# Early gate weight transposes, bias rows, and long rows for four divided zero fills, in a decode backward kernel

## The chip, the cores and the metric

The kernel runs on one core of one Trainium2 chip. The metric is device time in microseconds (us); lower is better. There is a profile of one execution of each kernel.

A run is labelled "slow" where it takes over 1.5% longer than the fastest run of the same kernel.

## The reference

The reference is one decode step of attention and a gate, with all gradients. Cut to what matters:

```
xn = layernorm(x)                               # x: 2 x 1 x 512
s  = attention(xn @ wq, last 4096 keys) @ wo    # 32 query heads, 8 KV heads, cache of 32768 keys
g  = silu(relu(xn @ w1 + b1)**2 @ w2 + b2)      # gate: 512 -> 1792 -> 512
out = x + s * g
# returned: out and the gradients of x, k_cache, v_cache, wq, wo, w1, b1, w2, b2
```

The gradients of the two caches have the cache's full shape (2 x 8 x 32768 x 128 bf16, 134 MB each), but only the last 4096 of 32768 keys are used. The other seven eighths, 235 MB, are zeros that must be written. That is most of what the kernel does.

## The kernel before

Zeros are written by 31 "fills" of 7.34 MB issued from GpSimd and one last fill from SyncE. The source is a tile of `uint8` zeros, cast during the transfer. A row longer than 28,672 bytes is written as fp32, so that a row of 57,344 bytes still fits the source:

```
def zf(o, q, r0, nent, rows, rep=1):       # nent x rep rows of rows*256 bytes each
    ...
    w = rows * DH
    if w > ZG * DH:                        # ZG = 112, DH = 128
        v = v.bitcast(F32); w //= 2
    ...
    sw_fill.append(nc.gpsimd.dma_start(out=v, in_=zs))

zlong = (0, 1, 3, 5, 7, 9, 11, 12, 14, 16, ...)     # whole fills: 128 entries of 224 rows (57,344 B), 1 packet each
zshort = {                                          # divided fills: (entries, rows of 256 B, repeats); last piece: what remains, one row each
    2: ((5, 8, 2), (120, 68, 3), (128, 32, 1), (16, 1, 1)),
    4: ((3, 1, 2), (2, 99, 6), (128, 112, 1), (128, 102, 1), (86, 1, 1)),
    ...
    13: ((2, 20, 2), (3, 30, 2), (128, 112, 1), (128, 109, 1), (124, 1, 1)),
    ...
}
```

Loads go out from SyncE: w1, w2, wo, wq, then the first V. The first K load shares its buffer with w1 and w2, so it waits until the gate weights have been transposed, which the old kernel does last in its prologue:

```
b1_bf = pw.tile([P, FK], BF16); dma_store.dma_start(out=b1_bf[:], in_=B_b1.rearrange("(p j) -> p j", j=FK))
b2_bf = pw.tile([P, DK], BF16); dma_store.dma_start(out=b2_bf[:], in_=B_b2.rearrange("(p k) -> p k", k=DK))
...   # layer norm, gate, dS;  do = dS @ wo.T;  q = xn @ wq
jobs = [...]                              # 112 transposes of w1 and w2 into w1T, w2T
...
knat = load(A_k_cache, 0, "k")            # the buffer of w1 and w2
for r in range(NR):                       # 4 rounds
    scores(dp_ps, vnat, zdo); scores(s_ps, knat, zq)
    ...                                   # softmax, its gradient
    outer_store(p_bf, bddo, vnat, out_3, r);  vnat = load(A_v_cache, r + 1, "v")   # dV written over V, stored
    outer_store(ds_bf, bdq, knat, out_2, r);  knat = load(A_k_cache, r + 1, "k")   # dK likewise
```

So in each round the next V (or K) can be loaded only when the gradient in the same buffer has been stored. At the end come the weight gradients; SyncE stores `out_8`, then `out_6`, and only then issues the last fill:

```
last = nc.sync.dma_start(out=out_6..., in_=dw1_st)
with tc.issue_after(last.ins):
    fin = nc.sync.dma_start(out=v, in_=zs)     # also waits for the last but one software fill
```

## Time and profile before

| | before |
|---|---|
| time, median | 765.2 us |
| span of the profiled run | 763.3 us |
| bytes moved, mean rate | 326.73 MB, 428 GB/s |
| PE, DVE, ACT busy | 51%, 36%, 28% |

The page of the kernel before: its span, the busy time and share of each engine, then two rows of 40 equal time slices (DMA in tenths busy, and GB/s), and the DMA packets.

```profile
span 763.3 us, 9400 instructions
PE 387.6 (51%) x4118; PEld 233.5 (31%) x4118; DVE 275.8 (36%) x483; ACT 214.6 (28%) x313; POOL 34.0 (4%) x67
DMA  9999999999999999999999999999999999999998
GB/s 382 443 416 422 451 412 425 444 435 416 430 432 450 416 439 429 426 427 446 414 431 435 437 428 427 429 433 440 425 436 437 432 434 422 428 441 425 422 428 379
DMA packets 11833, 326.73 MB, mean 428 GB/s; under 512 B 2898, under 2 KB 2906, under 8 KB 2934
```

No compute engine is near full; the DMA engines are, in every slice but the last. The GB/s jump from slice to slice; spread over their own durations, the packet records give 423 to 435 GB/s in every 10 us from 10 to 760 us.

What SyncE waited for before its first K load, in the view of waits (us in total, times, longest):

```profile
SPq L210 <- PE tp L345: 82.9, 1, 82.9
```

And why the layer norm starts so late, in the timeline (the bracket has the idle time before, and what ended it):

```profile
20.52 0.17 DVE L248 CAST b2T<-b_bf 128x4 f32<-128x4 bf16 x1 [8.93 <-DMA b_bf<-in_B_b_dram]
20.82 1.86 PE L158 MATMUL pp<-xT_f,ones_f 128*128 128x2 f32 x8 [12.72 <-DVE goT L244]
```

VectorE stands still for 8.93 us until a bias of 1 KB has landed in 128 pieces of 8 bytes.

### The profile page before, as it was taken

Reading aid. Unit: us, or ns where it says so; the run is one execution under the profiler, and the core shown is the slowest. Engines: PE = TensorE matmul, PEld = TensorE weight load, DVE = VectorE, ACT = ScalarE, POOL = GpSimd, SP = SyncE. Lnnn points to the kernel's source line nnn. Section 1 sums busy time; section 2 is a strip of 40 time slices with the busy share of each in tenths; the row PEclk is TensorE's granted clock in tenths of the full one; section 3 lists DMA queues with packets and bytes.
Section 4 is the critical chain, followed back from the end, with each engine's and each line's share of the span. In section 5 each row is a group of like instructions: output and inputs, shape, how many; then the busy total and the mean of one; then the engine's idle time right before and its main releaser. Section 6 shows DMA issues by size and latency. Waiting matters only on the chain.

```text
span 763.3 us, 9400 instructions
## 1 busy us (share of the span) xinstructions
PE 387.6 (51%) x4118; PEld 233.5 (31%) x4118; DVE 275.8 (36%) x483; ACT 214.6 (28%) x313; POOL 34.0 (4%) x67
## 2 busy tenths in 40 slices
PE   0666774477003648850576673015073775866800
PEld 0533553333002435420244430014053343423200
DVE  3333342485002347540344653003045152666600
ACT  0144521455000244540112553002013231722500
POOL 0200100010000000000000000000000000000000
PEclk9987997778556886775578587559585675855555
DMA  9999999999999999999999999999999999999998
GB/s 382 443 416 422 451 412 425 444 435 416 430 432 450 416 439 429 426 427 446 414 431 435 437 428 427 429 433 440 425 436 437 432 434 422 428 441 425 422 428 379
DMA packets 11833, 326.73 MB, mean 428 GB/s; under 512 B 2898, under 2 KB 2906, under 8 KB 2934
## 3 DMA queue, kind: packets, MB, share of 16 engines
q0 software_dynamic: 7360, 227.55, 70.5%
q1 hardware_dynamic: 2696, 56.63, 20.9%
q10 hardware_dynamic: 1736, 41.95, 13.2%
q8 instruction: 32, 0.52, 0.3%
q14 instruction: 9, 0.07, 0.0%
HBM read 45.62 MB, written 280.50 MB: 427 GB/s over the span
## 4 chain that ended last, share of the span: by engine, by line
DMA 36%; PE 31%; DVE 12%; ACT 9%; issue 6%; ACTq 0%; DVEq 0%; SPq 0%
DMA nat<-in_A_k_cache_dram 18%; DMA out_dram<-nat 15%; PE ov L421 7%; PE tp L387 4%; ACT nat L150 3%; ACT p_bf L455 2%; DMA b_bf<-in_B_b_dram 2%; PE ps L410 2%; DVE nat L152 2%; ACT tring L150 2%; DVE ds_bf L468 2%; PE s_ps L394 2%; PE wps L588 2%; PE dops L314 2%; PE tp L310 1%
## 5 line engine op out<-in xcount | busy, mean ns | idle before, releaser
L387 PE MATMUL tp<-pperm,nat 128*128 128x128 bf16 x1024 | 91.8, 242 | 180.0 <-DMA nat<-in_A_v_cache_dram 130.0
L152 DVE COPY tring<-tp 128x1024 bf16<-128x1024 bf16 (+1 forms) x98 | 66.1, 689 | 211.0 <-PE tp L387 201.8
L387 PEld LDWEIGHTS <-nat 128*128 128x128 bf16 x1024 | 68.4, 109 | 200.1 <-DMA nat<-in_A_v_cache_dram 131.9
L150 ACT COPY tring<-tp 128x1024 bf16<-128x1024 bf16 (+1 forms) x34 | 34.4, 1011 | 260.2 <-PE tp L387 235.5
L150 ACT CAST nat<-ov 128x512 bf16<-128x512 f32 x160 | 87.4, 590 | 63.6 <-PE ov L421 62.8
L152 DVE CAST nat<-ov 128x512 bf16<-128x512 f32 x96 | 65.5, 690 | 54.3 <-PE ov L421 51.8
L101 POOL DMA_DIRECT2D out_dram<-zt x58 | 32.5, 565 | 529.1 <-DMA out_dram<-zt 507.8
L421 PE MATMUL ov<-bd,ds_bf 128*128 128x512 bf16 x128 | 48.6, 455 | 5.7 <-DVE nat L152 3.7
L421 PE MATMUL ov<-bd,p_bf 128*128 128x512 bf16 x128 | 48.7, 452 | 4.2 <-DVE nat L152 1.4
L410 PE MATMUL ps<-t,nat 128*128 128x16 bf16 x1024 | 28.7, 173 | 14.5 <-issue 7.6
L410 PEld LDWEIGHTS <-nat 128*128 128x128 bf16 x1024 | 28.7, 102 | 17.3 <-issue 12.2
L394 PEld LDWEIGHTS <-zz 128*32 128x32 bf16 x512 | 17.4, 94 | 34.0 <-issue 24.0
L152 DVE CAST wq<-wps 128x512 bf16<-128x512 f32 x16 | 11.0, 690 | 44.2 <-PE wps L581 44.0
L394 PE MATMUL s_ps<-tring,zz 128*32 128x256 bf16 x256 | 19.9, 299 | 12.0 <-ACT tring L150 6.9
L402 PE MATMUL tp<-ident_bf,p_bf 128*128 128x128 bf16 x64 | 7.5, 312 | 34.9 <-ACT p_bf L455 34.9
L150 ACT CAST wq<-wps 128x512 bf16<-128x512 f32 x16 | 9.4, 585 | 53.3 <-PE wps L581 53.3
L455 ACT ACTIVATE p_bf<-e_sb,rl 32x512 bf16<-32x512 f32 x16 | 22.8, 1424 | 3.4 <-DVE rl L452 3.3
L394 PE MATMUL dp_ps<-tring,zz 128*32 128x256 bf16 x256 | 19.4, 305 | 7.7 <-ACT tring L150 4.6
L468 DVE SCALAR_TENSOR_TENSOR ds_bf<-dp_ps,delta,p_bf 32x512 bf16<-32x512 f32 x16 | 21.7, 1359 | 0.2
L421 PEld LDWEIGHTS <-ds_bf 128*128 128x128 bf16 x128 | 12.9, 107 | 20.4 <-issue 17.9
L421 PEld LDWEIGHTS <-p_bf 128*128 128x128 bf16 x128 | 12.8, 109 | 19.8 <-issue 17.1
L402 PEld LDWEIGHTS <-p_bf 128*128 128x128 bf16 x64 | 6.5, 146 | 36.0 <-ACT p_bf L455 36.0
(195 smaller groups left out, 444.4 us busy)
## 6 DMA issues: line engine op xcount, KB each, us to landing
out_dram<-zt POOLq DMA_DIRECT2D x23, 7168.0 KB, 96.7
out_dram<-nat ACTq DMA_DIRECT2D x8, 4096.0 KB, 40.9
out_dram<-zt POOLq DMA_DIRECT2D x7, 3584.0 KB, 71.1
nat<-in_A_v_cache_dram SPq DMA_DIRECT2D x4, 4096.0 KB, 33.8
nat<-in_A_k_cache_dram SPq DMA_DIRECT2D x4, 4096.0 KB, 31.6
out_dram<-zt SPq DMA_DIRECT2D x1, 7168.0 KB, 37.4
out_dram<-zt POOLq DMA_DIRECT2D x2, 3488.0 KB, 64.0
out_dram<-zt POOLq DMA_DIRECT2D x1, 6120.0 KB, 67.4
```

Source lines behind the costliest of these rows:

```text
L101: sw_fill.append(nc.gpsimd.dma_start(out=v, in_=zs))
L150: nc.scalar.copy(out=out_ap, in_=in_ap)
L152: nc.vector.tensor_copy(out=out_ap, in_=in_ap)
L314: nc.tensor.matmul(dops[0:B, :, :], lhsT=dsT_bf[:, dk, :], rhs=woT[:, :, dk, :], start=(dk == 0), stop=(dk == DK - 1))
L387: nc.tensor.transpose(tp[:, j, :], nat[:, g * CC + half * CH + j, :], pperm[:].rearrange("p b k -> p (b k)"))
L394: nc.tensor.matmul(out_ps[pr * RB:(pr + 1) * RB, half * CH * PB:(half + 1) * CH * PB], lhsT=zbuf[:, pr, o:o + RB], rhs=tT[:, :, pr, :], st ...
L402: nc.tensor.transpose(tp[:, cc, :], src[:, half * CH + cc].rearrange("r k b -> r (k b)"), ident_bf[:, :])
L410: nc.tensor.matmul(ps[:], lhsT=nat[:, g * CC + half * CH + cc, :], rhs=cols[half][:, cc, :, g, :], start=(half == 0 and g == 0 and cc == 0 ...
L421: nc.tensor.matmul(ov[:], lhsT=src[:, cc].rearrange("r k b -> r (k b)"), rhs=bd[:, gh * 4:(gh + 1) * 4, :], start=True, stop=True)
L455: nc.scalar.activation(out=p_bf[rb, :, :, pr], in_=e_sb[rb], func=ACT.Copy, scale=rl[rb, 0:1])
L468: nc.vector.scalar_tensor_tensor(out=ds_bf[rb, :, :, pr], in0=dp_c[rb], scalar=delta[rb, 0:1], in1=p_bf[rb, :, :, pr], op0=ALU.subtract, o ...
L588: nc.tensor.matmul(wps[:], lhsT=o_rows[:, j:N:NJ], rhs=ds_rows[:, :], start=True, stop=True)
```

## The change

It does three things: it loads the biases as single rows and adds them by one-row matmuls; it transposes the gate weights before the `do` and `q` work, which frees the first K buffer; and it writes the main part of fills 4, 6, 13 and 20 in one transfer of 55 KB rows where there were two of at most 28 KB. The core of the diff:

```
-        4: ((3, 1, 2), (2, 99, 6), (128, 112, 1), (128, 102, 1), (86, 1, 1)),
-        6: ((3, 1, 2), (3, 53, 2), (128, 112, 1), (128, 109, 1), (60, 1, 1)),
+        4: ((3, 1, 2), (2, 99, 6), (128, 214, 1), (86, 1, 1)),
+        6: ((3, 1, 2), (3, 53, 2), (128, 221, 1), (60, 1, 1)),
-        13: ((2, 20, 2), (3, 30, 2), (128, 112, 1), (128, 109, 1), (124, 1, 1)),
+        13: ((2, 20, 2), (3, 30, 2), (128, 221, 1), (124, 1, 1)),
-        20: ((4, 25, 2), (128, 112, 1), (128, 110, 1), (56, 1, 1)),
+        20: ((4, 25, 2), (128, 222, 1), (56, 1, 1)),
 ...
-        b1_bf = pw.tile([P, FK], BF16, name="b1_bf")
-        dma_store.dma_start(out=b1_bf[:], in_=B_b1.rearrange("(p j) -> p j", j=FK))
+        b1_row = pw.tile([1, F], BF16, name="b1_row")
+        dma_store.dma_start(out=b1_row[:], in_=B_b1.rearrange("(b f) -> b f", b=1))
 ...                                       # b2 likewise; the copies b1T, b2T go
-                                 start=(k == 0), stop=(k == DK - 1))
+                                 start=(k == 0), stop=False)
+            nc.tensor.matmul(hps[:, fk, :], lhsT=b1_row[:, fk:F:FK], rhs=one_row[:], start=False, stop=True)
 ...                                       # the block "jobs = [] ..." moves up, ahead of "do_rows = ..."
```

More of the change, by code (lines that the diff above doesn't have):

```diff
@@ L217 @@
         dma_store.dma_start(out=go_bf[:], in_=grad_out.rearrange("b s d -> (b s) d"))
-        b1_bf = pw.tile([P, FK], BF16, name="b1_bf")
-        dma_store.dma_start(out=b1_bf[:], in_=B_b1.rearrange("(p j) -> p j", j=FK))
-        b2_bf = pw.tile([P, DK], BF16, name="b2_bf")
-        dma_store.dma_start(out=b2_bf[:], in_=B_b2.rearrange("(p k) -> p k", k=DK))
+        b1_row = pw.tile([1, F], BF16, name="b1_row")
+        dma_store.dma_start(out=b1_row[:], in_=B_b1.rearrange("(b f) -> b f", b=1))
+        b2_row = pw.tile([1, D], BF16, name="b2_row")
+        dma_store.dma_start(out=b2_row[:], in_=B_b2.rearrange("(b d) -> b d", b=1))
+        one_row = pw.tile([1, B], BF16, name="one_row")
+        nc.vector.memset(one_row[:], 1.0)
         dma_load.dma_start(out=w1, in_=B_w1.rearrange("(p k) f -> p k f", k=DK))
@@ L244 @@
         nc.vector.tensor_copy(out=goT[:], in_=tp[:])
-        b1T = pw.tile([P, FK], F32, name="b1T")
-        nc.vector.tensor_copy(out=b1T[:], in_=b1_bf[:])
-        b2T = pw.tile([P, DK], F32, name="b2T")
-        nc.vector.tensor_copy(out=b2T[:], in_=b2_bf[:])
         meanb = pw.tile([P, B], F32, name="meanb")
@@ L269 @@
                 nc.tensor.matmul(hps[:, fk, :], lhsT=w1[:, k, fk:F:FK], rhs=xnT[:, k, :],
-                                 start=(k == 0), stop=(k == DK - 1))
-        hBT = pw.tile([P, FK, B], F32, name="hBT")
-        nc.vector.tensor_tensor(out=hBT[:], in0=hps[:], in1=b1T[:].unsqueeze(2).to_broadcast([P, FK, B]),
-                                op=ALU.add)
-        nc.vector.tensor_scalar_max(out=rT[:], in0=hBT[:], scalar1=0.0)
+                                 start=(k == 0), stop=False)
+            nc.tensor.matmul(hps[:, fk, :], lhsT=b1_row[:, fk:F:FK], rhs=one_row[:], start=False, stop=True)
+        nc.vector.tensor_scalar_max(out=rT[:], in0=hps[:], scalar1=0.0)
         nc.vector.tensor_tensor(out=h2T_bf[:], in0=rT[:], in1=rT[:], op=ALU.mult)
@@ L279 @@
                 nc.tensor.matmul(ups[:, dk, :], lhsT=w2[:, fk, dk:D:DK], rhs=h2T_bf[:, fk, :],
-                                 start=(fk == 0), stop=(fk == FK - 1))
+                                 start=(fk == 0), stop=False)
+            nc.tensor.matmul(ups[:, dk, :], lhsT=b2_row[:, dk:D:DK], rhs=one_row[:], start=False, stop=True)
         uT = pw.tile([P, DK, B], F32, name="uT")
-        nc.vector.tensor_tensor(out=uT[:], in0=ups[:], in1=b2T[:].unsqueeze(2).to_broadcast([P, DK, B]),
-                                op=ALU.add)
+        nc.vector.tensor_copy(out=uT[:], in_=ups[:])
         enu = pw.tile([P, DK, B], F32, name="enu")
@@ L300 @@
         nc.vector.tensor_copy(out=pk_rows(ds_rows[:]), in_=tp[:])
+        jobs = []
+        for fk in range(FK):
+            for k in range(DK):
+                jobs.append((w1[:, k, fk:F:FK], w1T, fk, k * P))
+        for dk in range(DK):
+            for fk in range(FK):
+                jobs.append((w2[:, fk, dk:D:DK], w2T, dk, fk * P))
+        for g0 in range(0, len(jobs), 8):
+            grp = jobs[g0:g0 + 8]
+            tp = ps_t.tile([P, 8, P], BF16, tag="pt")
+            for j, (src, _, _, _) in enumerate(grp):
+                nc.tensor.transpose(tp[:, j, :], src, ident_bf[:, :])
+            j = 0
+            while j < len(grp):
+                dst, idx, off = grp[j][1], grp[j][2], grp[j][3]
+                n = 1
+                while j + n < len(grp) and grp[j + n][1] is dst and grp[j + n][2] == idx and grp[j + n][3] == off + n * P:
+                    n += 1
+                evac(dst[:, idx, off:off + n * P], tp[:, j:j + n, :].rearrange("p a b -> p (a b)"))
+                j += n
         do_rows = pw.tile([B, N], BF16, tag="rows")
@@ L332 @@
         nc.vector.tensor_copy(out=qT_all[:], in_=tp[:])
-        jobs = []
-        for fk in range(FK):
-            for k in range(DK):
-                jobs.append((w1[:, k, fk:F:FK], w1T, fk, k * P))
-        for dk in range(DK):
-            for fk in range(FK):
-                jobs.append((w2[:, fk, dk:D:DK], w2T, dk, fk * P))
-        for g0 in range(0, len(jobs), 8):
-            grp = jobs[g0:g0 + 8]
-            tp = ps_t.tile([P, 8, P], BF16, tag="pt")
-            for j, (src, _, _, _) in enumerate(grp):
-                nc.tensor.transpose(tp[:, j, :], src, ident_bf[:, :])
-            j = 0
-            while j < len(grp):
-                dst, idx, off = grp[j][1], grp[j][2], grp[j][3]
-                n = 1
-                while j + n < len(grp) and grp[j + n][1] is dst and grp[j + n][2] == idx and grp[j + n][3] == off + n * P:
-                    n += 1
-                evac(dst[:, idx, off:off + n * P], tp[:, j:j + n, :].rearrange("p a b -> p (a b)"))
-                j += n
     kvt = attn.enter_context(tc.tile_pool(name="kvt", bufs=1))
```

## The prediction

> **What bounds the kernel now.** The DMA engines, in every stage. The page shows 326.73 MB at a mean 428 GB/s in a span of 763.3 us, the DMA row at nine tenths or more in 39 of 40 slices; PE is 51% busy, DVE 36%, ACT 28%. The Trainium skill ("DMA: Bandwidth & Descriptors", section "Where 436 GB/s comes from") gives a core's fabric ceiling as 435 GB/s; the trace agrees: its packet records, spread over their durations, give 425 to 435 GB/s in every 10 us from 10 to 760 us. The only losses are the first 4 us (nothing moves before 1.8 us) and the last 2 us, where the engines end between about 760 and 762 us. At 431 GB/s all bytes take 758 us. The chain of waits agrees: compute waits for K loads (27 to 49 us each) and stores of the same buffer (37 to 41 us).
>
> **What the change removes, adds and moves.**
> - Fills 4, 6, 13, 20: 8 issues of 128 rows become 4, 512 packets fewer. Packets of 28,672, 27,904 and 26,112 bytes take a mean 1080, 1056 and 988 ns, those of 57,344 bytes 2154 ns. By scaling, a pair (2068 to 2150 ns) becomes one row about 10 ns shorter; eight per engine and fill: some 0.1 us a fill, 0.3 to 0.4 us in all (estimate).
> - Biases: 256 packets of 28 and 8 bytes go. They take 9 ns each, but eight per engine queue behind packets of 14 to 33 KB: the second bias lands at 20.5 us, and DVE holds back the layer norm until then. Packet time saved: about 0.15 us. The layer norm should start near 9 to 12 us, not 20.8.
> - Eighteen one-row bias matmuls replace two adds: under 1 us on PE, off the bound.
> - The 112 gate weight transposes run before the do and q work. They free the K buffer: the first K load is issued near 35 to 55 us, not 94.4 (SyncE waits 82.9 us there). But V's load, ahead of it, lands only at about 75 us, so K lands near 95 to 105 us, not 123. Attention runs some 20 us earlier (12 to 32).
>
> **How much lies on the critical path.** Almost none of those 20 us: the fills take whatever time loads and stores leave, so an earlier load takes turns from fills, which end later. SyncE's final fill still waits for the last but one software fill and ends the kernel. What counts is packet time, about 0.5 us.
>
> **Balance of the engines.** The odd pieces (2 to 5 row groups) load single engines on purpose. The skill (same page, "Why a DMA increments its semaphore by 16 and not by 1") says a software DMA on fewer than 16 engines takes consecutive ones from a round-robin cursor; no view of this trace shows the engine. Had four 16-engine issues moved that cursor, engines would end apart: one piece is 6 packets of 0.95 us, so up to 5 us of tail. I think they don't move it.
>
> **Predicted:** 764.6 us, range 763.3 to 766.2; faster by over 2%: 0.01, within 2%: 0.98, slower by over 2%: 0.01.
>
> **Right if:** about 11,000 packets; mean rate 428 to 429 GB/s; K's first load lands about 20 us earlier; the last software fill lands later than 727 us; compute ends earlier, yet the span moves under 1 us. **Wrong if:** a gap in the DMA row, or a last slice well below 379 GB/s (balance lost).
>
> **What would make it wrong.** A moved cursor (2 to 5 us slower); a fill queue that runs dry late; a tail that the change balances better (1 to 2 us faster).

## More of the kernel before

SyncE's DMA issues in order of time (start in us, duration, engine and line, destination and source), cut to the first K load, each round's V load, and the last two:

```profile
95.46 0.53 SPq L210 DMA_DIRECT2D nat<-in_A_k_cache_dram  x1
202.67 0.54 SPq L210 DMA_DIRECT2D nat<-in_A_v_cache_dram  x1
336.93 0.54 SPq L210 DMA_DIRECT2D nat<-in_A_v_cache_dram  x1
482.61 0.54 SPq L210 DMA_DIRECT2D nat<-in_A_v_cache_dram  x1
...
724.57 0.33 SPq L639 DMA_DIRECT2D out_dram<-dw  x1
725.00 0.42 SPq L644 DMA_DIRECT2D out_dram<-zt  x1
```

These lines are a clock for compute: the store of `dw` (out_6) is issued when compute is done, here at 724.57 us. Compute therefore ends 39 us before the profiled span does.

## The result

| | before | after |
|---|---|---|
| median, 6 runs each | 765.17 us | 764.88 us |
| lowest to highest | 765.05 to 765.32 | 764.80 to 765.01 |
| ratio of the fast runs | | 0.9997, 95% interval 0.9984 to 1.0009 |

A ratio is the mean time of one kernel's fast runs over that of the other's fast runs of the same rounds, so not quite the ratio of the medians. The two sets of six runs do not overlap, but their distance, 0.3 us, is within the interval of the ratio.

The page after, the same rows:

```profile
span 763.0 us, 9422 instructions
PE 398.6 (52%) x4127; PEld 242.3 (32%) x4136; DVE 274.7 (36%) x481; ACT 216.7 (28%) x314; POOL 32.0 (4%) x63
DMA  9999999999999999999999999999999999999998
GB/s 382 439 424 437 410 443 434 435 423 433 419 436 440 419 440 434 427 426 431 431 429 443 431 431 422 432 430 445 426 436 437 431 434 434 415 432 434 421 426 378
DMA packets 10973, 326.73 MB, mean 428 GB/s; under 512 B 2548, under 2 KB 2557, under 8 KB 2586
```

860 packets are gone, the bytes and the rate are the same, the last slice has 378 GB/s against 379: the engines' balance held. The layer norm starts at 10.71 us, not 20.82, and the first K load waits 26.4 us, not 82.9 (timeline; then waits of SyncE):

```profile
10.71 1.87 PE L158 MATMUL pp<-xT_f,ones_f 128*128 128x2 f32 x8 [0.26 <-DVE goT L246]
```

```profile
SPq L210 <- PE tp L309: 26.4, 1, 26.4
```

SyncE's issues after:

```profile
38.97 0.54 SPq L210 DMA_DIRECT2D nat<-in_A_k_cache_dram  x1
192.40 0.54 SPq L210 DMA_DIRECT2D nat<-in_A_v_cache_dram  x1
339.91 0.54 SPq L210 DMA_DIRECT2D nat<-in_A_v_cache_dram  x1
487.26 0.54 SPq L210 DMA_DIRECT2D nat<-in_A_v_cache_dram  x1
...
726.72 0.33 SPq L635 DMA_DIRECT2D out_dram<-dw  x1
727.14 0.41 SPq L640 DMA_DIRECT2D out_dram<-zt  x1
```

Here is the surprise. The first K load is issued 56 us earlier and its data ends at 85.8 us, not 121.7. Round 1's V load is still 10 us ahead. Round 2's is 3 us behind, round 3's 5 us behind, and compute ends at 726.72 us, 2 us *later* than before. The head start is gone, and the time of the kernel does not show it at all. Two questions follow: where did the lead go, and does it matter when compute ends?

Most of the 36 us by which K's data comes earlier was never a lead of compute. In the kernel before, TensorE (PE) stood still for the first K for only 9.3 us (waits of PE, before, 60 to 200 us):

```profile
PE tp L387 <- DMA nat<-in_A_k_cache_dram: 9.3, 1, 9.3
```

It came from the q work and the gate transposes only at 96.18 us and then had V's transposes and scores to do; after, it starts on V at 86.43 us and waits for K no longer. The lead to follow is that of round 0's first store, 14.5 us (165.2 against 179.7 us, packet records). It was not lost to slower matmuls either: the profiled run's mean granted clock fell from 0.699 to 0.683 and PE's busy time grew by 11 us, but in the matmuls of the rounds it went only from 257 to 259 us (six groups of the view of lines, added up; 9 of 2816 records are missing after). Most of the growth, 8 us, lies in the prologue.

**Where the lead went.** The store of dV of round 1 in both kernels: the DMA queues in just the window of that store (q10 carries the stores, q0 the software fills; packets, MB, share of 16 engines). Before, 317 to 335 us:

```profile
DMA packets 285, 7.73 MB, mean 430 GB/s; under 512 B 33, under 2 KB 33, under 8 KB 33
q10 hardware_dynamic: 134, 4.13, 54.3%
q0 software_dynamic: 148, 3.56, 46.7%
```

After, 311 to 338 us:

```profile
DMA packets 367, 11.46 MB, mean 424 GB/s; under 512 B 101, under 2 KB 101, under 8 KB 108
q10 hardware_dynamic: 146, 4.29, 68.0%
q0 software_dynamic: 218, 7.12, 62.1%
```

The store has 128 packets of 32,768 bytes (the rest are small ones) and in both windows the rate is full. Beside it the fill queue moved 3.56 MB before and 7.12 MB after. The packet records say why: before, the fill packets in the window were rows of 27 KB (fill 13 in its old form), after, rows of 56,576 bytes. The queues take turns packet by packet, so a row twice as long takes twice the bytes at each turn. The Trainium skill ("DMA: Bandwidth & Descriptors", section "Issuing engines are not separate DMA queues") says that all issuers' transfers run on the same 16 engines and interleave; the section "Queues, rings and completion order" puts the switch at a packet. This trace agrees: from 40 to 50 us in the kernel after, 48 fill rows of 57,344 bytes and 48 load rows of 32,768 bytes were moved. From the same records, the store took 18.5 us before and 27.3 us after: (4.2 + 3.7) MB and (4.2 + 7.1) MB over some 427 and 414 GB/s. At its start 5.8 us of the lead were left, at its end the kernel was 2.9 us behind. So this store accounts for 8.7 us of the loss; the rest is not traced step by step.

This is theory A: **the new long rows spent the lead that the new prologue earned.** Rival B: the lead is lost whatever the rows are, because loads that come earlier simply meet other fills. For the time itself, the **packet theory** says that it is the sum of packet times and that the end of compute does not matter; its rival says that compute's end is a bound too.

### The profile page after: what moved, and what is told of

Its sections match the earlier page's. It is cut to its first block, busy times and chain, and to the rows that moved or that the text cites. A ratio compares the mean times of both kernels' runs of the same rounds, so it can differ in the third digit from the quotient of the medians.

```text
span 763.0 us, 9422 instructions
## 1 busy us (share of the span) xinstructions
PE 398.6 (52%) x4127; PEld 242.3 (32%) x4136; DVE 274.7 (36%) x481; ACT 216.7 (28%) x314; POOL 32.0 (4%) x63
## 2 busy tenths in 40 slices
DMA packets 10973, 326.73 MB, mean 428 GB/s; under 512 B 2548, under 2 KB 2557, under 8 KB 2586
## 4 chain that ended last, share of the span: by engine, by line
PE 34%; DMA 33%; DVE 12%; ACT 10%; issue 7%; ACTq 0%; DVEq 0%; SPq 0%
DMA out_dram<-nat 16%; DMA nat<-in_A_k_cache_dram 10%; PE ov L417 7%; PE tp L383 6%; DMA nat<-in_A_v_cache_dram 5%; ACT tring L150 3%; ACT p_bf L451 2%; ACT nat L150 2%; DVE nat L152 2%; PE ps L406 2%; PE s_ps L390 2%; DVE ds_bf L464 2%; PE wps L584 2%; PE dops L331 1%; DVE tring L152 1%
## 5 line engine op out<-in xcount | busy, mean ns | idle before, releaser
L101 POOL DMA_DIRECT2D out_dram<-zt x54 | 30.4, 567 | 531.3 <-DMA out_dram<-zt 510.1
L417 PE MATMUL ov<-bd,p_bf 128*128 128x512 bf16 x123 | 46.7, 447 | 5.5 <-ACT nat L150 1.4
L417 PEld LDWEIGHTS <-ds_bf 128*128 128x128 bf16 x128 | 13.4, 111 | 27.4 <-issue 25.6
```

What stands on the lines that cost most here:

```text
L417: nc.tensor.matmul(ov[:], lhsT=src[:, cc].rearrange("r k b -> r (k b)"), rhs=bd[:, gh * 4:(gh + 1) * 4, :], start=True, stop=True)
```

## The experiments

Twelve kernels ran, in three groups one after the other on the same chip, each group with runs of the kernel before beside it. "Compute ends" is SyncE's issue of the out_6 store in the profiled execution, one for each kernel. In the first group before had a median of 765.30 us (11 runs), in the second 765.24 (7), in the third 765.63 (9, from 765.05 to 766.07).

### The two halves apart: prologue_only and fills_only

The kernel after with the old table of fills; and the kernel before with the new table.

```
# prologue_only = after, with the old entries for 4, 6, 13, 20
# fills_only    = before, with the new entries for 4, 6, 13, 20
```

> The new prologue (early gate transposes, bias rows) with the old fills. Packet theory (the time is the sum of packet times, only packets removed save time): about 765.05 us, 0.1 to 0.15 us below before, from the bias packets alone. Where the early K load's lead went: theory A (rows of 55 KB take a larger share of turns on each engine from loads and stores than rows of 28 KB) says that with the old fills the 17 us lead of round 0 is largely kept: SyncE issues its last fill near 710 to 717 us against 725.0 before and 727.1 after. Rival B (the lead is lost whatever the rows, because loads that come earlier just meet other fills) says about 725 to 728 us here too.

> The old prologue with the new fills. Packet theory: 0.2 to 0.35 us below before, about 764.9 us. Theory A: compute ends some 10 to 15 us later than before, SyncE's last fill issues near 735 to 740 us, still without a dry DMA queue, so the time does not show it. Rival B: SyncE's last fill within 3 us of before's 725 us.

| | median | compute ends | round 1, 2, 3 V load issued |
|---|---|---|---|
| before (first profile) | 765.2 | 724.6 | 202.7, 336.9, 482.6 |
| after | 764.88 | 726.7 | 192.4, 339.9, 487.3 |
| prologue_only | 765.18 | 718.5 | 186.9, 331.6, 482.9 |
| fills_only | 765.54 | 733.6 | 203.4, 349.1, 493.2 |

The store of out_6 in prologue_only, then in fills_only:

```profile
718.52 0.33 SPq L635 DMA_DIRECT2D out_dram<-dw  x1
733.59 0.33 SPq L639 DMA_DIRECT2D out_dram<-dw  x1
```

The prologue alone makes compute end 6 us earlier, the long rows alone 9 us later, and together they nearly cancel. So A has the sign right. But A's number for prologue_only (710 to 717 us) was missed: SyncE's last fill came at 718.95 us, and of 16 us lead in round 1 nothing was left in round 3, with the old rows. A's number for fills_only (735 to 740 us) was just missed too, at 734.01 us. And each number is one profile: after's two differ by 1.8 us, and no_spacer below, which moves only 1.5 KB, ends compute 3.9 us earlier than after. B holds part of the truth: rounds also drift with what they meet.

The times are equal within the interval (ratios 0.9998 and 1.0001). The 0.2 to 0.35 us that the packet theory expected from the long rows did not show: fills_only's median was 0.24 us above before's. And one of fills_only's five executions took 790.46 us. That single run is slow and has no profile; it is set aside here.

### bias_only

Before, with only the bias rows and the bias matmuls:

```
-        b1_bf = pw.tile([P, FK], ...)           # and b2_bf, b1T, b2T
+        b1_row = pw.tile([1, F], ...)           # and b2_row, one_row; matmuls as in the change
```

> Before with only the bias rows and the bias matmuls (transposes in their old place, old fills). Packet theory: 0.1 to 0.15 us below before, as much as the whole new prologue. Rival: the saving of the new prologue comes from the earlier transposes, and this run equals before within 0.05 us. In the profile the layer norm's first sum starts near 8 to 11 us, not 20.8 us; the first K load issue moves from 95.5 us by less than 12 us.

The first K load was issued at 87.5 us, 8 us earlier than before. The time was a clear miss: one execution took 764.86 us, the other five, the profiled one among them, 781.69 to 786.78 us. They are slow, with a granted clock of 0.677 to 0.692 against 0.691 in the fast one. As one slow run had 0.692, a lower clock does not explain them. In the profiled slow one, stretch by stretch (busy time of each engine with the number of instructions, granted clock, share of the DMA engines, GB/s):

```profile
core 0: us, PE busy (x) PEld busy (x) DVE busy (x) ACT busy (x) POOL busy (x), PEclk, DMA share, GB/s
700.00:720.00 20.00, 13.13 (x67) 5.49 (x66) 12.47 (x18) 4.69 (x9) 0.00 (x0) 0.50 1.07 421
720.00:740.00 20.00, 14.27 (x42) 7.15 (x43) 12.78 (x19) 5.59 (x10) 0.00 (x0) 0.50 0.27 114
740.00:760.00 20.00, 14.80 (x35) 4.01 (x33) 11.17 (x18) 10.20 (x18) 0.00 (x0) 0.50 0.83 349
```

From 720 to 740 us the DMA engines have little to do (114 GB/s), while PE and DVE still compute. Compute ended at 756.9 us in this execution; the fills had run out before. By the packet records, its dK store of round 2 and the V load beside it had met fill packets of 57.3 KB in the mean, where those of the kernel before met 28 KB. With this the second bound is in sight: a **dry queue**. If compute ends too late, the fills that should hide it are used up. But these were slow runs, which prove nothing by themselves; the test is bias_all_short below.

### all_long and plain

After, with fills 2, 8, 10 and 15 in long rows as well; and after with every fill whole, without any odd pieces:

```
+        2: ((5, 8, 2), (120, 204, 1), (128, 32, 1), (16, 1, 1)),          # all_long
+        8: ((4, 82, 6), (128, 208, 1), (80, 1, 1)),                       # 10 and 15 likewise
```
```
+    zlong = tuple(range(31))                                              # plain
+    zshort = {}
```

> After with the main parts of fills 2, 8, 10 and 15 in long rows as well (624 packets fewer). Packet theory: about 0.3 us below after, 764.5 to 764.7 us, and the fastest so far. Theory A: compute ends later than in after (SyncE's last fill after 730 us). If compute then ends too late for the stores behind it, a gap would show near 735 to 745 us and the time would rise above after's; I expect no gap.

> After with every fill whole (128 rows of 57,344 bytes): no odd pieces that load some engines more than others. If these pieces balance the engines, the engines end at different times: the tail, in which the sum over engines falls from 430 GB/s to 0, grows from 2 us to some 8 to 16 us[...], and the time grows by 5 to 12 us, although there are fewer packets. The rival (they don't matter, only packets count) says 764.2 to 764.6 us.

all_long, which the packet theory made the fastest, took 784.10 and 785.53 us in its two fast runs (ratio 1.0254, interval 1.0237 to 1.0272) and 798 to 804 us in four more. plain took 807.27 to 811.72 us in four fast runs (ratio 1.0587, interval 1.0563 to 1.0612), with the fewest packets of all, 8684. all_long's expectation that compute would end later held (773.1 us, in a run labelled slow); its "no gap" failed, for by packet records all engines stood still from 740.3 to 759.7 us but for one moment. In plain, the tail was the wrong reason: its compute ended only at 784.8 us, when the last data of the software fills had been through since 709.0 us.

```profile
784.81 0.33 SPq L626 DMA_DIRECT2D out_dram<-dw  x1
```

Without divided fills every K and V transfer is beside 57 KB rows (24 to 33 us each in the packet records, from round 0's first store until the fills ran out).

So the short rows and the one-row remainders are not only a balance. They are a throttle on the fills: while a 256-byte remainder is served, a turn costs the loads next to nothing. (Row length is shown for all fills together; the remainders' part was not tested alone.) In the kernel before, from 350 to 355 us, the records have 30 fill packets of 256 bytes, 33 load packets and 32 store packets: equal turns, and hardly a byte for the fills.

### one_fill_less

After without fill 30, wrong (output 3 holds no zeros there):

```
-        for qi in range(ZQ - 1):
+        for qi in range(ZQ - 2):
```

> Wrong on purpose: fill 30 (7.34 MB of zeros) is left out. If bytes through the DMA engines are the whole bound, the time falls by 7.34 MB over 431 GB/s = 17.0 us, to about 747.9 us. If the end of compute is a bound too, it falls by less.

The median was 751.74 us, the profiled run 750.38 us: less gained than 17.0 us. The profiled span fell by 14.4 us (763.0 to 748.6). The trace shows the rest as idle time of the DMA engines: 2.7 us in the mean of the 16 between 700 and 720 us (shares of 0.82 and 0.91 below), and by packet records all of them stood still from 709.4 to 711.4 us. The stretches of that run:

```profile
core 0: us, PE busy (x) PEld busy (x) DVE busy (x) ACT busy (x) POOL busy (x), PEclk, DMA share, GB/s
700.00:710.00 10.00, 10.00 (x24) 3.22 (x23) 7.47 (x12) 6.45 (x11) 0.00 (x0) 0.50 0.82 354
710.00:720.00 10.00, 8.72 (x21) 2.37 (x20) 6.35 (x10) 5.66 (x10) 0.00 (x0) 0.50 0.91 390
```

Bytes are the bound, but only for the first 14 us or so; then compute is.

### all_short and bias_all_short

After with every fill in rows of at most 28,672 bytes; and bias_only with the same fills:

```
+    zlong = ()                     # and the old entries of zshort
```

> After with all fills in rows of at most 28 KB, the old form, also those that were whole (some 3,450 packets more than after). Packet theory: a pair of 28,672-byte packets takes some 6 ns longer than one of 57,344 bytes, 8 per engine and fill, 23 fills: about 1.1 us, plus 0.3 us for the four fills put back: 766.0 to 766.6 us. Theory A: loads and stores get a clearly larger share beside the fills (53% instead of 36% when one load runs), so K and V loads land in some 20 to 28 us instead of 38 to 40, and SyncE's last fill issues before 690 us. A rival that holds compute to be the bound says the time falls by over 5 us with it.

> The kernel of bias_only with every fill in rows of at most 28 KB, nothing else. In bias_only most executions took 782 to 787 us and one 764.9 us; the profiled slow one shows the DMA engines without work for some 19 us around 724 to 743 us, while compute still runs until 757 us. Theory (dry queue): the fills ran out before compute ended, since compute's loads and stores got too few turns beside rows of 57 KB; with short rows compute ends before 700 us, the fills last until the final fill, and all executions take 765.5 to 766.2 us. Rival (a slow state of the chip that has nothing to do with the fills): executions over 780 us appear here too.

all_short took 765.85 us (765.71 to 765.94), and its compute ended 85 us earlier than after's:

```profile
641.84 0.33 SPq L635 DMA_DIRECT2D out_dram<-dw  x1
729.01 0.39 SPq L640 DMA_DIRECT2D out_dram<-zt  x1
```

The loads beside fills alone took 14.9 to 19.8 us by packet records, not the 17.4 to 28.0 us of after. The last fill, which the expectation took as the clock (before 690 us), came only at 729.01 us, as it also waits for the last but one software fill. A kernel whose compute ends 85 us earlier is no faster than before in the same group, its median even 0.6 us higher: the theory that compute is the bound falls for this range. What packets cost was over-estimated (766.0 to 766.6 us expected) and is not resolved: against prologue_only, which differs only in the fills but ran in another group, 2,944 more packets, 184 per engine, go with 0.67 us, or 3.6 ns each; yet the interval of the ratio to before (0.9992 to 1.0022) holds no change too, and bias_all_short, with as many packets, had a median only 0.2 us above before's.

bias_all_short took 765.83 to 766.14 us in all five executions, none slow. Only the fills differ from bias_only. The dry queue stands.

### transposes_only

Before, with only the block of gate transposes moved up:

```
+        jobs = [] ...              # ahead of do_rows
         do_rows = pw.tile(...)
```

> Before with only the early gate transposes (element-wise bias loads, old fills). The first K load is issued 40 to 65 us after the start instead of 95.5 us, because the transposes still have to wait until the bias has landed at 20 us or not at all; the packets are those of before, so the time of its steady executions is 765.1 to 765.4 us, equal to before. Open: how much of round 0's lead is left at the end; by prologue_only (SyncE's last fill at 719.0 us) 0 to 10 us earlier than before's 725.0 us.

```profile
45.31 0.54 SPq L210 DMA_DIRECT2D nat<-in_A_k_cache_dram  x1
694.83 0.33 SPq L639 DMA_DIRECT2D out_dram<-dw  x1
722.79 0.39 SPq L644 DMA_DIRECT2D out_dram<-zt  x1
```

Here the whole lead survived and grew: compute ended 30 us earlier than before. SyncE then sat until the last but one software fill was in, and issued the last fill at 722.79 us. The time: 765.63 us, and before's median in the same group: 765.63 us (ratio 0.9999). This is the cleanest evidence that compute's end is worth nothing here. It also shows how loosely the rounds are coupled to the prologue: prologue_only, with the bias rows besides, kept 6 us of lead, this one 30.

### fill13_short

After with fill 13 alone back in short rows:

```
+        13: ((2, 20, 2), (3, 30, 2), (128, 112, 1), (128, 109, 1), (124, 1, 1)),
```

> After with fill 13 alone put back to two pieces of 28 KB rows. Theory (a share by turns): the store of round 1's dV, which ran beside fill 13 for 18.5 us in before (27 KB rows) and 27.3 us in after (rows of 56 KB), takes 18 to 21 us again; the K and V loads of round 2 are issued some 6 to 9 us earlier than in after (339.9 and 375.3 us). Rival (the rounds drift for other reasons): the store stays near 27 us. Time: 764.9 to 765.1 us, that is after plus at most 0.1 us of packets, since compute's end is not the bound.

The store of round 1's dV took 22.5 us by packet records (27.3 in after, 26.8 in its second profile below), a bit more than expected. Round 2's loads came 8.8 and 7.3 us earlier, as expected in size; of the 8.8 us, the shorter store gives 4.8, and 3.0 were there before, as the store began at 307.9 us and not 310.9:

```profile
331.13 0.54 SPq L210 DMA_DIRECT2D nat<-in_A_v_cache_dram  x1
368.01 0.54 SPq L210 DMA_DIRECT2D nat<-in_A_k_cache_dram  x1
```

So the share by turns (A) is right for the transfers beside this fill. But compute ended at 727.2 us, as late as after's: later rounds met other fills and lost it again (B). Both are at work. The time, 764.90 us, is after's.

### no_spacer

After without the first small piece of fill 4:

```
-        4: ((3, 1, 2), (2, 99, 6), (128, 214, 1), (86, 1, 1)),
+        4: ((2, 99, 6), (128, 214, 1), (92, 1, 1)),
```

> After without the first small piece of fill 4 (3 rows of 256 bytes, twice); its rows go to the remainder piece, 1.5 KB in all. If pieces on fewer than 16 engines take consecutive engines from a cursor, all later odd pieces land 3 engines off, the balance is lost, and the time grows by 2 to 8 us with a longer tail. If there is no cursor, the time stays within 0.1 us of after.

Two 256-byte rows on three entries went elsewhere, 1.5 KB in all, and the time rose to 769.23 us (ratio 1.0052, interval 1.0035 to 1.0068) although compute ended at 722.8 us, earlier than after's. The tail shows it. First no_spacer, then after:

```profile
755.00:760.00 5.00, 0.00 (x0) 0.00 (x0) 0.00 (x0) 0.00 (x0) 0.00 (x0) 0.50 0.80 341
760.00:766.00 6.00, 0.00 (x0) 0.00 (x0) 0.00 (x0) 0.00 (x0) 0.00 (x0) 0.50 0.33 141
```

```profile
755.00:760.00 5.00, 0.00 (x0) 0.00 (x0) 0.00 (x0) 0.00 (x0) 0.00 (x0) 0.50 0.98 421
760.00:766.00 6.00, 0.00 (x0) 0.00 (x0) 0.00 (x0) 0.00 (x0) 0.00 (x0) 0.58 0.12 53
```

Both have the last fill alone to move by then. In no_spacer some engines are idle before 760 us while others work until 766; in after nearly all work until 760. This is what a cursor would do that hands small transfers to consecutive engines, as the Trainium skill states ("DMA: Bandwidth & Descriptors", section "Why a DMA increments its semaphore by 16 and not by 1"). No view names the engine of a packet, so the cursor itself is inferred. (The remainder piece changed from 86 to 92 entries too, which may move it as well.)

### after_again

The changed kernel a second time, beside the third group.

> The changed kernel unchanged, a second time, on the same chip as the other runs of this call. Packet theory: 0.2 to 0.4 us below before. No execution over 766 us, as compute ends some 13 us before the stores behind it run out (about 740 us); if that slack is smaller than the spread between executions, some executions are slow.

Four executions took 764.67 to 764.83 us, a fifth 766.19 us, so "none over 766 us" was missed by one run; nothing of it is known. The ratio to before is 0.9992 (0.9979 to 1.0004), before being slower in this group than in the others. Compute ended at 728.5 us.

### The two bounds in one table

| kernel | time of the profiled run | compute ends | difference |
|---|---|---|---|
| all_short | 765.71 | 641.8 | |
| bias_all_short | 765.95 | 651.8 | |
| transposes_only | 765.81 | 694.8 | |
| prologue_only | 765.22 | 718.5 | |
| before | 765.12 | 724.6 | |
| after | 764.80 | 726.7 | |
| fills_only | 765.54 | 733.6 | |
| bias_only (slow) | 782.49 | 756.9 | 25.6 |
| all_long (slow) | 798.68 | 773.1 | 25.6 |
| plain | 810.79 | 784.8 | 26.0 |
| one_fill_less | 750.38 | 724.7 | 25.6 |

Once the fills have run out, the kernel ends 25.6 to 26.0 us after compute: the last stores and the last fill, which is issued behind them. Otherwise it ends when all bytes are through, near 765 us. So the time is the larger of the two, and the corner lies at 765 - 25.6, about 739 us (worked out from this table). After has 11 to 13 us of room before that corner (728.5 and 726.7 us in its two profiles); one_fill_less, whose bytes end some 17 us earlier, is beyond it.

No version beat both kernels clearly. fill13_short is equal to after within 0.2 us in the same group. all_short's median is about 0.7 us over that of prologue_only, from another group, and it has about 100 us of room.

## Why the prediction was right or wrong, point by point

- **The bound and the time: right.** 764.6 us was predicted, 764.88 us measured. Bytes through the DMA engines bound both kernels, and transposes_only showed that a lead of 30 us is worth nothing. Part of the hit was luck: the prediction did not know the corner at 739 us, and compute moved towards it, not away from it.
- **Packet time, about 0.5 us: not resolved.** Measured: 0.3 us in the first comparison, 0.9 us in after_again, where before itself was 0.4 us slower than in the other groups. Neither interval excludes zero. The halves don't show it either: prologue_only's median was 0.1 us below before's, fills_only's 0.24 us above. Where packets were added in bulk (all_short), the comparison gives 3.6 ns for each on its engine (bias_all_short against before: 1.3 ns), where the records of before (2 x 1080 against 2154 ns) had suggested 6 ns, so the expectation for all_short was 0.2 to 0.8 us too high.
- **About 11,000 packets, 428 GB/s, a last slice near 379 GB/s: right** (10,973; 428; 378).
- **Bias matmuls under 1 us on PE: wrong, and without effect.** 14 took 213 ns each and 4 took 188 ns, 3.7 us if added up.
- **Layer norm at 9 to 12 us, K issued at 35 to 55 us: right** (10.71 and 38.97 us).
- **K lands near 95 to 105 us: wrong, 85.8 us.** The step was "V's load, ahead of it, lands only at about 75 us". V's last data packet had ended at 65.6 us; I had read its completion records, which stand at 74 to 76 us in before and at 66 to 70 us in after.
- **"Attention runs some 20 us earlier (12 to 32)" and "compute ends earlier": the first held only for the start (14.5 and 10.3 us in round 0 and 1), the second was wrong.** Round 0's dV store began 14.5 us earlier (165.2 against 179.7 us), round 1's V load 10.3 us earlier; then compute fell behind and ended 2 us later. The missing step was that the same change doubles the length of rows on the fill queue, and with it the fills' bytes per turn beside loads and stores. I had costed the rows' own time and not their effect on their neighbours.
- **"The last software fill lands later than 727 us": wrong**, for the same reason: its packets ended at 725.0 us, against 727.2 before. The fills took more turns' worth of bytes, not fewer.
- **"The fills take whatever time loads and stores leave": the wrong picture.** Beside loads and stores they take a share that goes with row length (3.56 against 7.12 MB in the windows above), and loads and stores have the rest. It came to the same time because compute stayed inside its room.
- **The balance was kept without the four transfers: right** (378 against 379 GB/s in the last slice). It doesn't show that they left the cursor alone: a cursor that goes round 16 engines is back in its place after a transfer on all 16. no_spacer showed that a lost balance costs 4 us; that a cursor lost it is inferred.
- **"A fill queue that runs dry late"** was named as a risk. It does not happen in before or after, but half of the change alone comes near it: fills_only ended compute at 733.6 us and had one execution of five at 790 us (no profile of that one), so the prologue and the long rows seem to belong together. That the 790 us run was a dry queue is only argued.

Left open: why one execution of bias_only escaped and five did not, as only a slow one was profiled; and what exactly makes the rounds drift, so that compute's end differs by 24 us between transposes_only and prologue_only and by 62 us between transposes_only and the slow bias_only. That the fills met decide it is shown for one store (fill13_short) and for all fills together (all_short, plain), not round by round.

## What to carry to other kernels

When two streams share the DMA engines and one is only there to fill time, the length of its rows can set how much it takes from the other: here long rows were at best a little cheaper in packets and much dearer for the neighbour. Before making compute earlier in a kernel bound by bytes, read two numbers from the profile: when compute ends, and how late it could end before the transfers behind it no longer fit; inside that room nothing is gained, beyond it every microsecond is lost. A change of two parts that barely moves the time may consist of one part that earns and one that spends, so run the halves alone, and look at every execution and not only at the median.

## What the Trainium skill lacked or had wrong

- "DMA: Bandwidth & Descriptors", section "Queues, rings and completion order", has queues switching at packets, without saying what follows for bandwidth: with one row per packet record here, a queue's share goes with its row length. The same 4.2 MB store took 18.5 us beside 27 KB rows and 27.3 us beside rows of 56 KB.
- The same page's advice on size (section "Rules for kernel authors") is about a transfer by itself. Here the step from 28 KB to 57 KB rows was worth at most some 3.6 ns per saved packet per engine, 0.67 us in the whole kernel and not clear of noise, while the effect on neighbouring transfers moved compute's end by 77 us (all_short against prologue_only).
- Section "Why a DMA increments its semaphore by 16 and not by 1" has the round-robin cursor but not what a balance built on it is worth. Moving 1.5 KB of small pieces cost 4 us here (769.23 us), if the cursor is the cause; four fewer transfers on all 16 engines left the tail as it was (378 against 379 GB/s in the last slice).
- No page gives a delay as long as the 9 us by which a load's completion trails its data here, beside other transfers: V's last data packet ended at 65.6 us and its completion records stand at 74 to 76 us in before, where nothing followed it on its queue; with K queued behind it, in after, they stand at 66 to 70 us. I have no explanation.
- Section "Where 436 GB/s comes from" agreed on the ceiling: 435 GB/s stated, 423 to 435 GB/s in every 10 us here. Its remark that for transfers between HBM and SBUF the HBM side, about 358 GB/s, binds does not hold for this kernel, which ran on one core: 428 GB/s in the mean over 326.73 MB, nearly all between HBM and SBUF.
